# Residual of pairs 1 to 3 and the last pair's q/k transposes by DMA, with a frozen job order

## The chip, the core and the metric

The kernel runs on one core of one Trainium2 chip. The metric is the device time of one execution in microseconds (us); most executions of one kernel agree within about 1% here. TensorE does the matrix products, VectorE (DVE), ScalarE (ACT) and GpSimd (POOL) the elementwise work, SyncE (SP) issues nearly all DMA transfers. TensorE's work is in two forms: 128x128 tiles for the dense layers and four 64x64 tiles for attention.

## The reference

```python
# attention without softmax: batch 8, heads 8, sequence 576, head size 64
scores = q @ k^T / sqrt(64)
out    = (scores * D_h) @ v        # D_h[t,s] = gamma_h**(t-s) for t>=s, else 0
x = out with heads side by side    # 8 x 576 x 512
# gated layer
h = gelu(x @ w_in)                 # 512 -> 1024
u, v = two halves of h
v_n = layernorm(v) * g_ln
v_s = w_sg @ v_n + b_sg            # product along the sequence, 576 x 576
result = x + (u * v_s) @ w_out     # the residual is this "x +"
```

All inputs and the output are float32; the kernel works in bfloat16 on TensorE.

## The kernel before

The eight batches are handled as four **pairs**, a pair as nine row tiles of 128 rows, hence 36 output tiles. Attention goes through five blocks per pair (four of 256 rows, one of 128), 20 in all, and carries a state from block to block. For each block: transposes of q and k (job T), scores (S), state (Z) and attention output (O), which gives `xT`, the transposed x. For each row tile: the v half (hv) and the u half (hu) of the first dense layer; for each batch the spatial product with `w_sg` (wp); for each tile the output product (op).

Every piece is a job with an engine, an estimated duration and a due time. A planner in Python places them when the program is built: on each engine it takes, of the jobs that can start at about the earliest time, the one that is due first. The chip then runs each engine strictly in that order.

```python
    def a_OS(b, g):                      # attention output of block b, with scores of the next in it
        a_O(b, st.pop((b, "zs")))
        cur.pop("mark", None)
        if g is None:
            nc.tensor.drain()
        else:
            a_S(b + 1, g)
            nc.tensor.drain()
        cur.pop("mark", None)
        a_O2(b)                          # the last 8 matmuls, into banks that the first part also writes

    def m_U(i):                          # one tile, 16 matmuls of N=128
        ...
        for c in range(KK):
            for kk in range(KK):
                nc.tensor.matmul(hu[:, c, :], w_in[:, kk, 128 * c:128 * c + 128],
                                 xTs[p][:, kk, 128 * m:128 * m + 128],
                                 start=(kk == 0), stop=(kk == KK - 1), skip_group_check=True)

    def m_O(i):                          # output tile i
        ...
        for j in range(KK):              # the residual: xT transposed back by a product with the identity
            nc.tensor.matmul(o6[:, j // 2, :, j % 2, :], xTs[p][:, j, r], ident[:].rearrange("p (c d) -> p c d", c=2),
                             start=(j == 0), stop=False, skip_group_check=True)
        for c in range(KK):
            nc.tensor.matmul(op[:], gTs[p][:, c, r], w_out[:, c, :], start=False, stop=(c == KK - 1),
                             skip_group_check=True)

    def m_Oev(i):
        nc.scalar.activation(cur["ob", i][:], cur.pop(("op", i))[:], Act.Copy)
    ...
    loads(0)                             # q, k, v of block 0
    jv = [win_load(1, 0), win_load(1, 1)]
    ju = [win_load(0, 0), win_load(0, 1)]
    loads(1)
    loads(2)
    sg = [sg_load(j) for j in range(SB)]
    loads(3)
    wo = [wo_load(0), wo_load(2)]
    for b in range(4, NBL):
        loads(b)
```

## Time and profile before

| before | value |
|---|---|
| first three timed runs, median (range) | 241.68 us (240.2 to 243.03) |
| span of the profiled run | 239.6 us |
| TensorE busy | 215.4 us, 90% |
| first wp | 61.32 us |
| first wp to last matmul | 61.3 to 235.8, 174.5 us |

The busy times of the engines, the stretches of 20 us, the chain and the middle of TensorE's timeline are shown in the prediction below. What it does not show is the DMA part of the page; the second line is packets, MB and the time of the packets as a share of 16 engines' span:

```profile
DMA packets 70765, 42.92 MB, mean 179 GB/s; under 512 B 14817, under 2 KB 63993, under 8 KB 70721
...
q1 hardware_dynamic: 70176, 42.26, 63.4%
```

To read: over the span the main queue fills 63% of the DMA engines' time. That average hides how full they are at each time: 0.89 to 1.05 in the stretches up to 80 us, 0.12 to 0.15 from 160 to 220 us.

### The profile page before, as it was taken

What the parts mean: (1) busy time and instruction counts of PE and PEld (TensorE: products, weight loads), DVE (VectorE), ACT (ScalarE), POOL (GpSimd) and SP (SyncE); (2) the same over time, 40 slices, a digit from 0 to 9 for tenths busy, and PEclk for the clock granted to TensorE, in tenths of its full rate; (3) what the DMA queues carried; (4) which work ended last, traced back from release to release, by engine and by line L of the source; (5) the groups of instructions that cost most, each with busy time, mean ns of one, the idle gap of its engine ahead of it and who ended that gap; (6) DMA issues with size and microseconds to landing.
All of it is one profiled execution on the core that took longest, in us unless ns stands there. A gap on an engine that the chain in (4) does not pass through costs nothing.

```text
span 239.6 us, 10051 instructions
## 1 busy us (share of the span) xinstructions
PE 215.4 (90%) x4440; PEld 148.0 (62%) x4485; DVE 137.1 (57%) x230; ACT 135.1 (56%) x234; POOL 126.8 (53%) x198
## 2 busy tenths in 40 slices
PE   7975839887989999999999999899999999999993
PEld 2442617654766676677676667566757666667761
DVE  7991626665765745665667466374756555634420
ACT  2027247865656475576645665767473656865422
POOL 8955645499595569772437497906083802221000
PEclk9999989999999999999999999999999999999998
DMA  6999589999899985898564658971110220111324
GB/s 177 251 237 259 138 260 328 290 277 267 176 302 280 310 219 149 244 294 238 149 196 137 193 140 253 298 198 47 48 47 11 80 94 34 59 47 44 131 92 175
DMA packets 70765, 42.92 MB, mean 179 GB/s; under 512 B 14817, under 2 KB 63993, under 8 KB 70721
## 3 DMA queue, kind: packets, MB, share of 16 engines
q1 hardware_dynamic: 70176, 42.26, 63.4%
q8 instruction: 35, 0.57, 1.1%
q10 hardware_dynamic: 544, 0.02, 0.2%
q14 instruction: 10, 0.07, 0.1%
HBM read 32.80 MB, written 9.44 MB: 176 GB/s over the span
## 4 chain that ended last, share of the span: by engine, by line
PE 76%; DMA 13%; issue 4%; ACT 3%; SPq 1%; POOL 1%; ACTq 0%
PE wp L575 17%; PE hu L559 13%; PE op L596 13%; PE hv L517 12%; PE pp L439 7%; DMA ld<-in_q_dram 4%; PE pp L367 4%; PE pp L393 4%; PE op L593 3%; DMA ld<-in_moe_w_out_dram 3%; DMA ld<-in_moe_w_in_dram 3%; PE zp L421 3%; DMA ld<-in_moe_w_sg_dram 2%; ACT xT L506 1%; PE scr L248 1%
## 5 line engine op out<-in xcount | busy, mean ns | idle before, releaser
L403 DVE TENSOR_TENSOR ret<-pp,msk 128x1024 bf16<-128x1024 f32 x32 | 38.9, 1220 | 27.8 <-PE pp L393 27.6
L350 POOL TENSOR_TENSOR qkb<-ld,gqv 128x512 bf16<-128x512 f32 x36 | 37.1, 1051 | 15.6 <-DMA ld<-in_q_dram 12.9
L350 POOL TENSOR_TENSOR vb<-ld,gqv 128x512 bf16<-128x512 f32 x36 | 38.2, 1081 | 5.8 <-DMA ld<-in_v_dram 3.6
L575 PE MATMUL wp<-wT,vn 128*128 128x288 bf16 x256 | 41.2, 286 | 0.0
L582 DVE TENSOR_TENSOR gT<-wp,uT 128x288 bf16<-128x288 f32 x64 | 28.7, 453 | 21.0 <-PE wp L575 20.8
L533 POOL TENSOR_SCALAR mv<-mv 128x2 f32<-128x2 f32 (+1 forms) x20 | 4.5, 226 | 67.5 <-DVE mv L529 48.9
L559 PEld LDWEIGHTS <-w_in 128*128 128x128 bf16 x576 | 34.4, 98 | 6.9 <-issue 0.3
L559 PE MATMUL hu<-xT,w_in 128*128 128x128 bf16 x576 | 38.3, 219 | 0.2 <-issue 0.2
L517 PE MATMUL hv<-w_in,xT 128*128 128x512 bf16 x122 | 35.6, 380 | 2.6 <-ACT xT L506 1.4
L528 DVE BATCH_NORM_STATS2 bst<-vg 128x6 f32<-128x512 f32 x36 | 24.8, 690 | 19.3 <-ACT vg L521 19.3
L596 PE MATMUL op<-w_out,gT 128*128 128x512 bf16 x127 | 33.4, 379 | 0.9
L521 ACT ACTIVATE vg<-hv 128x512 f32<-128x512 f32 x36 | 21.5, 596 | 20.3 <-PE hv L517 18.1
L600 ACT ACTIVATE ob<-op 128x512 f32<-128x512 f32 x36 | 21.4, 595 | 19.4 <-PE op L596 19.4
L372 DVE COPY qkT<-pp 128x2048 bf16<-128x2048 bf16 (+1 forms) x20 | 22.2, 1111 | 15.1 <-PE pp L367 15.1
L565 ACT ACTIVATE uT<-hu 128x512 bf16<-128x512 f32 x36 | 21.5, 596 | 15.6 <-PE hu L559 15.6
L548 ACT ACTIVATE vn<-vg,mv 128x512 bf16<-128x512 f32 x32 | 25.0, 809 | 8.8 <-POOL mv L536 8.7
L506 ACT ACTIVATE xT<-pp 128x512 bf16<-128x512 f32 (+1 forms) x40 | 24.6, 665 | 8.2 <-PE pp L439 8.2
L575 PEld LDWEIGHTS <-vn 128*128 128x128 bf16 x256 | 23.9, 98 | 6.7
L517 PEld LDWEIGHTS <-xT 128*128 128x128 bf16 x144 | 12.6, 98 | 13.1 <-ACT xT L506 2.4
L341 POOL CAST qkb<-ld 128x1024 bf16<-128x1024 f32 (+1 forms) x20 | 19.5, 975 | 0.5 <-DMA ld<-in_k_dram 0.5
L248 PE MATMUL scr<-warm 128*128 128x512 bf16 x61 | 17.6, 436 | 2.2 <-DVE warm L221 1.2
L421 PE MATMUL zp<-vb,qkb 64*64 64x64 bf16 x480 | 13.8, 194 | 6.1 <-ACT zb L427 4.4
(66 smaller groups left out, 263.9 us busy)
## 6 DMA issues: line engine op xcount, KB each, us to landing
out_dram<-ob SPq DMA_DIRECT2D x36, 256.0 KB, 2.7
ld<-in_q_dram SPq DMA_DIRECT2D x16, 512.0 KB, 5.5
ld<-in_k_dram SPq DMA_DIRECT2D x16, 512.0 KB, 6.9
ld<-in_v_dram SPq DMA_DIRECT2D x16, 512.0 KB, 8.1
ld<-in_moe_w_in_dram SPq DMA_DIRECT2D x8, 256.0 KB, 7.0
ld<-in_moe_w_sg_dram SPq DMA_DIRECT2D x4, 288.0 KB
ld<-in_q_dram SPq DMA_DIRECT2D x8, 128.0 KB, 5.1
ld<-in_k_dram SPq DMA_DIRECT2D x8, 128.0 KB, 3.6
```

What stands on the lines that cost most here:

```text
L350: nc.gpsimd.tensor_tensor(dst[:, s], src[:, s], gqv[:, a, 2 * n + s, :].unsqueeze(2).to_broadcast([128, H, D]), op=Alu.mult)
L372: nc.vector.tensor_copy(st[b, "qkT"][:].rearrange("p c a k t -> p c (a k t)")[:, :, :w], st.pop((b, "tp"))[:].rearrange("p c a k s t -> p ...
L403: nc.vector.tensor_tensor(ret[:].rearrange("p r (k t) -> p (r k) t", k=2), sc[:].rearrange("p r (k t) -> p (r k) t", k=2), msk2[:].rearran ...
L506: nc.scalar.activation(dst, src, Act.Copy)
L517: nc.tensor.matmul(hv[:], xTs[p][:, kk, 128 * m:128 * m + 128], w_in[:, kk, F2:], start=(kk == 0), stop=(kk == KK - 1))
L521: nc.scalar.activation(vgs[i][:], cur.pop(("hv", i))[:], Act.Gelu_apprx_tanh)
L528: nc.vector.bn_stats(bst[:], vgs[i][:])
L548: nc.scalar.activation(vn[:], vg[:], Act.Identity, scale=mv[:, s, 2:3], bias=mv[:, s, 3:4])
L559: nc.tensor.matmul(hu[:, c, :], w_in[:, kk, 128 * c:128 * c + 128], xTs[p][:, kk, 128 * m:128 * m + 128], start=(kk == 0), stop=(kk == KK ...
L575: nc.tensor.matmul(ps[:], vns[t0 + j][e][:, 128 * c:128 * c + 128], wT[e][j][:, half * HS:(half + 1) * HS], start=(j == 0), stop=(j == SB ...
L582: nc.vector.tensor_tensor(gTs[p][:, c, col:col + HS], cur.pop(("wp", b, c, half))[:], uTs[p][:, c, col:col + HS], op=Alu.mult)
L596: nc.tensor.matmul(op[:], gTs[p][:, c, r], w_out[:, c, :], start=False, stop=(c == KK - 1), skip_group_check=True)
```

## The change

The intent is to take work off TensorE. The residual of pairs 1 to 3 (27 of 36 tiles) no longer goes through TensorE: a DMA transpose turns `xT` back and VectorE adds it as it evacuates the output product. The q/k transposes of the last pair (blocks 15 to 19) become DMA transposes too. Around this, the drain in the attention output is replaced by a wait on another job, hu is 256 wide, the start is rearranged, and the planner's greedy choice is replaced by a fixed list of 921 jobs (and seven groups of filler, matmuls on a tile of zeros) that stands in the kernel's text. The planner's time model now counts instruction fetch.

```diff
+FETCH = (7200.0, 4800.0)
+ORDER = (
+    '0 f9 1 2 6 111 83 7 f10 84 112 3 8 114 113 f5 115 17 87 81 118 120 278 116 9 279 119 12 280 f7 281 88 121 117 '
+    ... (33 lines)
+)
     def plan(self):
+        if ORDER:
+            return self.follow(ORDER)
...
-    BUFS = dict(ld=9, qkb=2, vb=3, qkT=2, ret=4, zb=4, xT=2, uT=2, gT=2, vg=3, mv=3, vn=10, ob=3,
+    BUFS = dict(ld=12, wst=2, qkb=2, vb=3, qkT=3, ret=4, zb=4, xT=2, uT=2, vg=3, mv=3, vn=10, ob=3, xr=3,
+    XP = 1          # from this pair on the residual goes by DMA
+    TB = 15         # from this block on q and k are transposed by DMA
...
+    def win_load(half):              # was four loads of 512 KB, in shared buffers, each issued in two halves
+            nc.sync.dma_start(wst["in", half][:, :, :F2],
+                              moe_w_in.rearrange("(j p) f -> p j f", p=128)[:, :, half * F2:(half + 1) * F2])
...
+    def a_TX(b):
+        st[b, "qkT"] = new("qkT", [128, 2048], BF)
+        nc.sync.dma_start_transpose(st[b, "qkT"][:, :ns * 1024].rearrange("p (g t) -> p g t", t=128),
+                                    st[b, "qkb"][:, :ns * 1024])
...
     def a_O2(b):
+        on = pend.pop(b)
+        if on is None:
+            nc.tensor.drain()
+        elif on:
+            nc.tensor.wait_ge(swap, on)      # set by a matmul of a job that the order put between a_O and a_O2
...
     def m_O(i):
+        if p < XP:
+            for j in range(KK):
+                ins = nc.tensor.matmul(op[:, 128 * j:128 * j + 128], xTs[p][:, m, j, :], ident[:], ...)
         for c in range(KK):
+            ins = nc.tensor.matmul(op[:], uTs[p][:, c, r], w_out[:, c, :], start=(p >= XP and c == 0), ...)
+    def m_X(i):
+        cur["xr", i] = new("xr", [128, KK, 128], BF)
+        nc.sync.dma_start_transpose(cur["xr", i][:], xTs[p][:, m].rearrange("p j r -> p (j r)"))
     def m_Oev(i):
+        if i // NT < XP:
+            ins = nc.scalar.activation(ob[:], op[:], Act.Copy)
+        else:
+            ins = nc.vector.tensor_tensor(ob[:], op[:], cur.pop(("xr", i))[:].rearrange("p j r -> p (j r)"), op=Alu.add)
...
-    jv = [win_load(1, 0), win_load(1, 1)]
-    ju = [win_load(0, 0), win_load(0, 1)]
-    loads(1)
+    jv = win_load(1)
+    loads(1)
+    ju = win_load(0)
     loads(2)
```

Left out: the planner's new duration model, the row constants (now through TensorE instead of four partitions of VectorE and small DMAs), the memsets that move to VectorE, and q and k of block 0 prepared by VectorE and ScalarE instead of GpSimd.

## The prediction

> **What bounds the kernel now.** I read the page's parts 1 and 2 first, then busy time in stretches of 20 us, then TensorE's timeline in the filled middle and in the first 62 us, then the chain of waits that ended last, for the start only.
>
> The engines over the whole span (busy us, share, instructions), and from the costliest groups the one that the change's name aims at:
>
> ```profile
> PE 215.4 (90%) x4440; PEld 148.0 (62%) x4485; DVE 137.1 (57%) x230; ACT 135.1 (56%) x234; POOL 126.8 (53%) x198
> ...
> L593 PE MATMUL op<-ident,xT 128*128 128x128 bf16 x144 | 13.9, 219 | 0.0
> ```
>
> TensorE is the only engine near full; the others stand at 53 to 57%. The 219 ns of one matmul is its length in the pipeline, not its cost.
>
> The same by stretches (busy us of 20 per engine, TensorE's granted clock, DMA share, GB/s):
>
> ```profile
> 0.00:20.00 20.00, 17.22 (x219) 8.26 (x223) 16.93 (x31) 4.62 (x7) 14.07 (x31) 1.00 0.99 230
> 20.00:40.00 20.00, 12.35 (x307) 8.63 (x309) 7.91 (x14) 10.90 (x19) 11.06 (x14) 0.91 0.89 230
> ...
> 100.00:120.00 20.00, 19.55 (x398) 13.53 (x402) 11.90 (x20) 14.22 (x24) 10.46 (x17) 1.00 0.80 239
> 120.00:140.00 20.00, 19.33 (x475) 13.96 (x480) 12.37 (x22) 11.79 (x22) 11.52 (x17) 1.00 0.54 156
> ...
> 160.00:180.00 20.00, 19.44 (x425) 13.82 (x427) 11.96 (x20) 12.17 (x21) 9.25 (x15) 1.00 0.12 43
> ```
>
> There are two regimes. Up to about 60 us the DMA engines are full and TensorE is not; of its 17.22 us in the first stretch most is filler (61 recorded matmuls on "warm", 17.6 us in all) that only keeps the clock up. From 60 us on TensorE is 97% busy and the DMA engines fall to 0.12.
>
> The chain that ended last, at the start (start us, length, what):
>
> ```profile
> 3.16 7.15 DMA ld<-in_moe_w_in_dram
> 10.31 0.02 issue
> 10.33 10.50 DMA ld<-in_q_dram
> ...
> 27.32 5.44 DMA ld<-in_moe_w_sg_dram
> ...
> 37.62 7.39 DMA ld<-in_moe_w_out_dram
> ...
> 53.33 1.43 issue
> ```
>
> The second block's q lands only at 20.83, behind 2 MB of w_in. The first spatial product (wp, "W") starts at 61.32 in TensorE's timeline. By then TensorE has done 7 hv jobs, 7 hu jobs, transposes of 5.5 blocks, the transposes of w_sg and their small products. At the filled-middle costs below that is about 28 us of work in 61 us: 33 us are lost at the start.
>
> The filled middle, TensorE alone (start, length with overlap, what):
>
> ```profile
> 110.45 0.39 PE L593 MATMUL op<-ident,xT 128*128 128x128 bf16 x4
> 110.68 1.03 PE L596 MATMUL op<-w_out,gT 128*128 128x512 bf16 x4
> 111.54 1.06 PE L559 MATMUL hu<-xT,w_in 128*128 128x128 bf16 x16
> 112.44 0.65 PE L575 MATMUL wp<-wT,vn 128*128 128x288 bf16 x4
> 112.92 0.29 PE L575 MATMUL wp<-wT,vmid 128*128 128x288 bf16 x1
> 113.14 0.31 PE L439 MATMUL pp<-qkT,zb 64*64 64x128 bf16 x8
> ```
>
> What counts is start to start: residual 110.45 to 110.68, 0.23 us; output product 0.86; hu 0.90; the five wp some 0.61; then about 0.1 is lost as the array turns from 128x128 to 64x64 tiles. One pair of batches takes 50.0 us: the same hv job starts at 95.90, 145.07 and 195.89.
>
> **What the Trainium skill says.** (1) "TensorE: Matmul & The Clock Gate", section "Back-to-back issue gap", gives a warm gap of N/2.4 + 2.5 ns: 56 ns at N=128, 216 at N=512. The trace agrees: 0.23 us for four of N=128, 0.86 for four of N=512. So making hu 256 wide instead of 128 should save nearly nothing in streaming (0.89 us per unit either way). (2) "DMA: Bandwidth & Descriptors", section "Latency and other measured facts", gives a DMA transpose 261 GB/s. No run before this change has such a DMA. (3) "Runtime: NRT & Kernel Launch", section "Instruction fetch mechanics": instructions come in blocks of 256 (16 KiB), the crossing "mostly hidden". The trace has 35 packets on the instruction queue, and 8972 TensorE instructions / 256 = 35.05: the count agrees. That it is hidden is less clear: at 53.33 TensorE stands for 1.43 us for "issue", in the middle of one job with the DMA engines full.
>
> **The change, part by part.** Counts are from the two instruction orders (8972 TensorE rows before, 6701 after).
>
> a) Residual. Of 36 output tiles 27 lose 4 matmuls: 27 x 0.23 = 6.2 us off TensorE, all in the filled part. In return 27 DMA transposes of 128 KB, and VectorE adds and evacuates instead of ScalarE. An estimate from skill place (2): 128 KB / 261 GB/s = 0.5 us, 13.5 us of DMA time in all, mostly after 110 us where the DMA share was 0.54 and less. VectorE takes 27 evacuations, estimated at 0.65 us from ScalarE's 0.60 for the same tile: +17.5 us; it loses 5 qkT evacuations (-5.5) and the 4-partition row arithmetic of the start (about -10, given back in part by memsets that move to it): roughly 144 us, no bound. ScalarE loses 27 x 0.595 = 16 us.
>
> b) q and k of the last pair. Four full blocks and a half one: 4.5 x 0.52 us (119.97 to 120.49 is one full set) = 2.3 us off TensorE. Their DMA transposes move 2.36 MB, an estimated 9 us at 261 GB/s.
>
> c) No more drain behind each attention output. Before, the output job, scores in the drain's shadow and the last 8 matmuls took 101.85 to 103.18 = 1.33 us; their columns alone, 4 tiles at a time at 2.4 GHz, are 0.85. Some 0.23 of the rest is the two turns of the array, so about 0.25 is drain. The new order puts another job (T, Z or S) there and waits on a semaphore of that job. 17 jobs in the filled part x 0.25 = 4.2 us.
>
> d) Fewer turns between 64-wide and 128-wide work: 106 before, 78 after by the orders. 28 x 0.11 = 3.1 us, of which about 2.4 in the filled part.
>
> e) The start. w_in comes as two 1 MB loads behind q and k of the second block, q and k of block 0 are prepared by VectorE and ScalarE beside GpSimd, the row constants go through TensorE instead of DVE on 4 partitions and tiny DMAs, the staging has buffers of its own. In the new order the first wp stands behind the transposes of block 4. q and k of block 4 are the 20th load; by then some 9.8 MB have been asked for. At the 230 GB/s of the first 40 us, from 2 us on, they land near 44 us; preparing them takes GpSimd 3 us (1.04 + 2.04 in the trace); then come about 4.5 us of TensorE work. That gives 49 to 51 us for the first wp; I take 49.5, against 61.3. This is the largest and least sure term: 11.8 us.
>
> The sum. From the first wp to the last matmul before: 61.3 to 235.8 = 174.5 us. Minus 6.2 (a), 2.3 (b), 4.2 (c), 2.4 (d); plus 1.9 because half the w_sg transposes and one set of q/k transposes now come after the first wp: 161.3. 49.5 + 161.3 = 210.8; plus the tail after the last matmul, unchanged (235.8 to 239.6 = 3.8): a span of 214.6. The timed median was 2.1 above the profiled span (241.7 against 239.6): 216.7, rounded to **216**.
>
> **Rivals.**
>
> *The DMA engines become the bound.* Up to 160 us the old run used about 141 us of full DMA time (the shares of eight stretches). Ahead of the last load the new queue has 15 stores, 9 residual transposes and 2.5 q/k transposes: some 149 us by the estimates above. The last block's scores are needed about 176 us in, by counting 32 us of TensorE work behind the last attention output. For: 149 of some 165 is tight, and I have no measured time of a DMA transpose; at half the page's rate it is 158. Against: the queue was idle a third of 100 to 140 us. It would cost 5 to 10 us: 222 to 226.
>
> *The start is bound by arrivals anyhow.* If first wp stays near 57 us, because loads of the same bytes take as long, the gain there is 4 us and the time 224. Against: of the 61 us, several are order (a zp job waited 4.07 us behind a ScalarE cast that waited for w_sg), not bytes.
>
> *A fixed order that fits badly.* The job order is a frozen list; where the chip differs from the author's durations each engine still waits in order, and TensorE stalls on evacuations. VectorE and ScalarE at 65% leave room, but I would give up 3 to 6 us: 219 to 222.
>
> *Better than summed.* 2271 fewer TensorE instructions, so 26 fetched blocks for 35, could remove most of the "issue" stalls, and the new start may overlap more: 208 to 211.
>
> **Range and chances.** The removals in the filled part (15 us) rest on measured spacings and I trust them to 4; the start to 6 either way; the DMA rival pulls up only. So 216, 208 to 226 in 8 of 10. Even if the whole start gain failed, 241.7 - 13 = 229 would be over 5% faster; only a DMA queue that is badly blocked makes it same. Faster 0.96, same 0.03, slower 0.01.
>
> **What would show it.** No residual matmul in 27 tiles, and a pair (same hv job to same hv job) at about 46 us, 44 in the last. The first wp near 49.5 us. TensorE idle under 1 us per 20 in the filled part, with no DMA named as releaser of the added matmul or of VectorE's output add. Transposes near 0.5 us of 16 engines each. A DMA share near 1 still at 160 us, or TensorE waiting for qkT or GpSimd for ld late, would say the first rival; waits spread over evacuations the third. Wrong overall if first wp is later than 56 us or a pair takes over 48.

## The result, and the profile after

| | before | changed |
|---|---|---|
| timed, median (range), 4 runs each | 240.94 us (238.7 to 243.03) | 214.78 us (213.73 to 215.84) |
| span of the profiled run | 239.6 us | 213.9 us |
| first wp | 61.32 us | 45.43 us |
| last matmul ends | 235.8 us | 209.3 us |
| DMA transposes | none | 27 of 128 KB, 4 of 512 KB, 1 of 256 KB |

The ratio is 0.8951, interval 0.8875 to 0.9027: faster. All ratios here are the mean time of one kernel's fast runs over that of the other's of the same rounds, so not quite the ratio of the medians quoted. Medians and ranges take in every execution, slow ones too; the ratios do not. Where a difference of ratios is given in us, it is multiplied by the median of the kernel before in the same rounds.

Two repeats in later sets gave 0.902 and 0.9026. The mean of the three, 0.8999, is called the **pooled ratio** below. It is needed for the first set of experiments, which has no run of the changed kernel; the three values come from different chips, and from the lowest to the highest of them is 1.8 us.

The page of the changed kernel: engines, DMA packets and the main queue, the new add on VectorE, and the two DMA transposes (median us from issue to landing).

```profile
PE 199.7 (93%) x3372; PEld 133.7 (63%) x3372; DVE 141.3 (66%) x261; ACT 123.2 (58%) x214; POOL 113.5 (53%) x157
...
DMA packets 94117, 48.64 MB, mean 227 GB/s; under 512 B 38202, under 2 KB 87362, under 8 KB 94082
...
q1 hardware_dynamic: 94064, 48.13, 93.9%
...
L771 DVE TENSOR_TENSOR ob<-op,xr 128x512 f32<-128x512 f32 x27 | 18.4, 689 | 11.9 <-PE op L755 11.4
...
xr<-xT SPq DMA_TRANSPOSE x27, 2.8
qkT<-qkb SPq DMA_TRANSPOSE x5, 5.9
```

TensorE's recorded busy time fell by 15.7 us (3.5 of them filler, 17.6 to 14.1) and VectorE's rose by 4.2. The surprise is the queue: 93.9% of 213.9 us is 200.9 us of engine time, against 151.9 (63.4% of 239.6) before: 49 us more, for some 6 MB more. Packets under 512 B rose by 23,385. The transposes account for nearly all of them: in pieces of 256 bytes they make 27 x 512 + 4.5 x 2048 = 23,040, and counted by size the packets of 256 bytes went from 12,288 to 35,328, which is 23,040 more.

Busy time by stretches, in the columns of the prediction's table:

```profile
0.00:20.00 20.00, 18.16 (x240) 9.75 (x241) 12.78 (x39) 7.23 (x10) 9.59 (x23) 1.00 0.99 277
20.00:40.00 20.00, 17.73 (x376) 11.87 (x373) 13.27 (x24) 17.32 (x33) 12.91 (x16) 1.00 1.09 267
...
100.00:120.00 20.00, 18.16 (x429) 13.06 (x427) 14.09 (x25) 11.76 (x22) 12.64 (x17) 1.00 0.92 248
120.00:140.00 20.00, 18.59 (x327) 12.79 (x320) 13.54 (x25) 11.33 (x20) 13.43 (x18) 1.00 1.18 220
140.00:160.00 20.00, 18.50 (x303) 12.09 (x302) 13.45 (x24) 10.91 (x20) 11.96 (x13) 1.00 1.10 195
```

Two things to see. In the first 40 us the DMA moves 277 and 267 GB/s, not the 230 of before. And from 100 to 160 us TensorE is idle for 4.75 us while the DMA share stands at 0.92 to 1.18 (it can pass 1 because the packets' times overlap).

Of those 4.75 us, 4.71 are three stalls, in TensorE's timeline (in brackets the idle time and what ended it; "issue" means that the profile shows nothing it waited for):

```profile
104.01 0.27 PE L595 MATMUL pp<-qkT,zb 64*64 64x128 bf16 x3 [1.84 <-issue]
...
127.14 1.02 PE L662 MATMUL hv<-w_in,xT 128*128 128x512 bf16 x4 [1.41 <-ACT uT L719]
...
155.39 0.32 PE L542 MATMUL pp<-qkT 64*64 64x64 bf16 x16 [1.46 <-DMA qkT<-qkb]
```

The third is a DMA transpose of q and k that came late. The first two name no DMA; whether they hang on one is for the experiments. In the two repeats the three stalls were 0.9 (two stalls together) and 0.7 for "issue", 1.4 and 1.4 for ScalarE, 1.3 and 0.5 for the transpose; the idle time from 100 to 160 us was 3.58 and 3.40 us.

SyncE's timeline shows a second cost, the time that an issue takes:

```profile
147.70 3.04 SPq L518 DMA_TRANSPOSE qkT<-qkb  x1
150.78 0.58 SPq L430 DMA_DIRECT2D ld<-in_k_dram  x1
151.48 3.42 SPq L764 DMA_TRANSPOSE xr<-xT  x1
```

A 128 KB transpose holds SyncE's queue for at least 1.19 us in this run (3.42 here) and a 512 KB one for 3.0 to 4.3. A plain transfer can be held up too (2.97 us for the load of q at 41.66), but the shortest store takes 0.34 us and the shortest load 0.37. Whatever stands behind a transpose in the order is issued that much later. From 120 to 160 us SyncE is issuing for 36.4 of 40 us, against 12.2 in the kernel before.

The start, in the chain that ended last:

```profile
26.64 6.93 DMA ld<-in_v_dram
...
37.26 1.86 POOL qkb L462
39.13 1.00 POOL qkb L456
...
40.17 0.64 PE pp L502 x32
...
45.59 1.23 PE wp L728 x10
```

Block 4's q and k are prepared from 37.2 us on and GpSimd does not wait for them: they were there. TensorE transposes them at 40.17; 5.3 us later the first wp starts at 45.43 (the chain's piece begins a little after it).

Last, the drain, in TensorE's timeline:

```profile
46.88 0.62 PE L595 MATMUL pp<-ret,vb 64*64 64x128 bf16 x32
47.43 0.64 PE L502 MATMUL pp<-ident,qkb 64*128 64x64 bf16 x32
48.00 0.31 PE L595 MATMUL pp<-qkT,zb 64*64 64x128 bf16 x8
```

Between the output's 40 matmuls and its last eight (48.00) lies a transpose job, and the last eight follow it without a bracket.

### The profile page after: what moved, and what is told of

Same layout as the page of the kernel before. It is cut to its first block, busy times and chain, and to the rows that moved or that the text cites. A ratio compares the mean times of both kernels' runs of the same rounds, so it can differ in the third digit from the quotient of the medians.

```text
span 213.9 us, 7830 instructions
## 1 busy us (share of the span) xinstructions
PE 199.7 (93%) x3372; PEld 133.7 (63%) x3372; DVE 141.3 (66%) x261; ACT 123.2 (58%) x214; POOL 113.5 (53%) x157
## 3 DMA queue, kind: packets, MB, share of 16 engines
q1 hardware_dynamic: 94064, 48.13, 93.9%
## 4 chain that ended last, share of the span: by engine, by line
PE 75%; DMA 7%; ACT 6%; POOL 4%; DVE 4%; issue 2%; SPq 0%; POOLq 0%; DVEq 0%
PE wp L728 16%; PE op L755 13%; PE hu L709 12%; PE hv L662 12%; PE pp L595 5%; PE scr L340 5%; DMA qkT<-qkb 4%; PE pp L542 3%; DMA ld<-in_v_dram 3%; PE pp L502 3%; PE zp L574 3%; ACT xT L651 2%; PE op L750 1%; DVE ret L555 1%; DVE ob L771 1%
## 5 line engine op out<-in xcount | busy, mean ns | idle before, releaser
L462 POOL TENSOR_TENSOR vb<-ld,gqv 128x1024 bf16<-128x1024 f32 (+1 forms) x20 | 34.6, 1731 | 14.2 <-DMA ld<-in_v_dram 14.2
L462 POOL TENSOR_TENSOR qkb<-ld,gqv 128x1024 bf16<-128x1024 f32 (+1 forms) x19 | 32.7, 1723 | 15.9 <-PE zp L574 11.8
L738 DVE TENSOR_TENSOR uT<-wp,uT 128x288 bf16<-128x288 f32 x64 | 27.9, 449 | 18.9 <-PE wp L728 18.8
L709 PE MATMUL hu<-xT,w_in 128*128 128x256 bf16 (+1 forms) x320 | 37.3, 262 | 0.7 <-ACT xT L651 0.7
L662 PE MATMUL hv<-w_in,xT 128*128 128x512 bf16 x144 | 36.4, 380 | 1.4 <-ACT uT L719 1.4
L755 PE MATMUL op<-w_out,uT 128*128 128x512 bf16 x144 | 35.9, 379 | 0.3 <-DVE uT L738 0.3
L709 PEld LDWEIGHTS <-w_in 128*128 128x128 bf16 x320 | 27.9, 98 | 7.6 <-issue 0.9
L719 ACT ACTIVATE uT<-hu 128x512 bf16<-128x512 f32 x36 | 21.2, 596 | 12.3 <-PE hu L709 12.2
L771 DVE TENSOR_TENSOR ob<-op,xr 128x512 f32<-128x512 f32 x27 | 18.4, 689 | 11.9 <-PE op L755 11.4
L583 ACT ACTIVATE zb<-zp 128x256 bf16<-128x256 f32 x32 | 12.2, 380 | 15.4 <-PE zp L574 15.2
L755 PEld LDWEIGHTS <-uT 128*128 128x128 bf16 x144 | 13.3, 98 | 12.4 <-DVE uT L738 0.9
L511 DVE COPY qkT<-pp 128x2048 bf16<-128x2048 bf16 (+1 forms) x15 | 16.7, 1113 | 6.3 <-PE pp L502 6.1
```

Source lines behind the costliest of these rows:

```text
L462: eng.tensor_tensor(dst, src, g.unsqueeze(3).to_broadcast(list(src.shape)), op=Alu.mult)
L662: ins = nc.tensor.matmul(hv[:], xTs[p][:, m, kk, :], w_in[:, kk, F2:], start=(kk == 0), stop=(kk == KK - 1))
L709: ins = nc.tensor.matmul(hu[:, n, :], w_in[:, kk, 128 * c:128 * c + 128], xTs[p][:, m:m + w, kk, :], start=(kk == 0), stop=(kk == KK - 1), ...
L719: unfence(nc.scalar.activation(uTs[p][:, c0:c1, 128 * m:128 * m + 128 * w], cur.pop(("hu", i, half))[:], Act.Gelu_apprx_tanh), ("U", i, half))
L738: ins = nc.vector.tensor_tensor(uTs[p][:, c, col:col + HS], cur.pop(("wp", b, c, half))[:], uTs[p][:, c, col:col + HS], op=Alu.mult)
L755: ins = nc.tensor.matmul(op[:], uTs[p][:, c, r], w_out[:, c, :], start=(p >= XP and c == 0), stop=(c == KK - 1), skip_group_check=True)
```

## The experiments

Twelve runs in three sets, each set timed beside the kernel before on one chip, but each set on another one (medians of the kernel before: 242.87, 241.23 and 240.11 us). The theory: the order and the start carry most of the gain; the residual by DMA is not free, because the DMA queue has no room where the order puts it. The rival: the parts that the title lists (residual and transposes by DMA) give the gain and the order is a detail.

### The residual without its DMA

```diff
     def m_X(i):
-        cur["xr", i] = new("xr", [128, KK, 128], BF)
-        nc.sync.dma_start_transpose(cur["xr", i][:], ...)
+        return
     def m_Oev(i):
-            ins = nc.vector.tensor_tensor(ob[:], op[:], cur.pop(("xr", i))[:]..., op=Alu.add)
+            ins = nc.vector.tensor_tensor(ob[:], op[:], warm[:], op=Alu.add)     # warm is zero
```

> The changed kernel without its 27 residual transposes and without residual matmuls for these tiles (VectorE adds a tile of zeros instead: a wrong result on purpose, same VectorE work). Theory A, TensorE sets the pace and the DMA transposes are hidden: same as the changed kernel, 214 to 215 us, since no TensorE work changes. Theory B, the DMA queue is a second bound (share 0.94 over the span, above 1 in most stretches to 160 us): the transposes' share goes and 2 to 6 us with it, 209 to 213 us.

Measured: median 212.0 us (210.91 to 212.62), ratio 0.8752, interval 0.868 to 0.8825. Results are wrong, as meant. Its page and its stretches:

```profile
q1 hardware_dynamic: 79376, 44.59, 79.3%
```

```profile
100.00:120.00 20.00, 20.00 (x440) 14.24 (x439) 15.94 (x26) 13.27 (x25) 14.52 (x17) 1.00 1.05 284
120.00:140.00 20.00, 19.89 (x342) 13.41 (x344) 13.62 (x25) 12.80 (x21) 11.98 (x18) 1.00 0.72 168
140.00:160.00 20.00, 20.00 (x372) 14.18 (x361) 14.25 (x28) 11.62 (x21) 14.79 (x17) 1.00 0.88 211
```

TensorE's idle time from 100 to 160 us falls from 4.75 to 0.11 us; all three stalls are gone. So all three hang on the 27 transposes, though only one named a DMA. Against the pooled ratio the transposes cost (0.8999 - 0.8752) x 242.87 = 6.0 us (4.8 to 6.7 by the lowest and highest of its three values). In DMA engine time, 79.3% of 208.8 is 165.6 us; 200.9 - 165.6 = 35.3 us more with the 27, **1.31 us for each one added**. That is the rise of the total, with what they do to the other packets' times, and not the time of one transpose by itself. The chain of cause can begin early: with the transposes, pair 1's first ones are issued from 66.9 us on, and between 86 and 96 us the DMA share is 0.98 where it is 0.71 without them; so the loads of the next blocks start from a queue that is already full. By how much the stalls come from engine time and by how much from the issue time on the queue, this run does not tell: it takes both away.

### The transposes doubled

```diff
     def m_X(i):
+        again = new("xr2", [128, KK, 128], BF)
+        nc.sync.dma_start_transpose(again[:], xTs[p][:, m].rearrange("p j r -> p (j r)"))
```

> Each of the 27 residual transposes is issued a second time, into a tile that nobody reads: 27 more of 128 KB. A (hidden): at most +1 us, 214 to 216. B (second bound): the added DMA time shows, +4 to +15 us, 219 to 230. The difference of the DMA queue's total busy time against the changed kernel also measures what one transpose costs: 0.5 us of 16 engines if the skill's 261 GB/s holds, about 1 us if my reading of the two traces is right.

Measured: 236.88 us (234.54 to 237.47), ratio 0.9767, interval 0.9675 to 0.9859. That is (0.9767 - 0.8999) x 242.87 = 18.7 us over the changed kernel, for 27 transfers whose results nobody reads, and more than the 4 to 15 us that theory B expected. Between 120 and 140 us:

```profile
120.00:140.00 20.00, 15.59 (x262) 9.99 (x262) 10.14 (x18) 10.77 (x20) 13.79 (x19) 0.91 0.95 181
```

The first 27 cost 6.0 us and the second 27 cost 18.7. Here the profile does name transposes: VectorE's output add waits 7.5 us for them in all, and ScalarE waits 4.7 us for one before it writes a new xT (there are two buffers), with TensorE 4.5 us behind it. Not all of that is waiting: TensorE's busy time rose from 199.7 to 206.8 us, 7.1 us, at a mean granted clock of 0.954 instead of 0.996 (0.91 in the stretch shown). The run was also to measure one transpose, 0.5 or about 1 us. The main queue takes 92.8% of 235.3 = 218.4 us, 17.5 more than 200.9, so **0.65 us for each one added**, half of what the removal gave. A quiet stretch agrees: from 181 to 184 us of the changed kernel the queue moves one transpose and one 256 KB store, and is 45.6% busy, 1.37 us for the two together. So 1.31 us is what a transpose adds in this kernel's full queue, not a fixed cost. SyncE is now issuing for 16 to 19 of every 20 us from 100 to 220 us, 77.8 us of the run for these 54. So the issue time on the queue is a suspect beside the engines' time; the two are not told apart.

### The residual back on TensorE

```diff
-    BUFS = dict(ld=12, ... xT=2, ...)
+    BUFS = dict(ld=11, ... xT=3, ...)         # the order needs xT longer; one load buffer pays for it
     def m_O(i):
-        if p < XP:
+        if p < NP:                             # residual matmuls in all 36 tiles
     def m_X(i):
+        return
     def m_Oev(i):
-            ... tensor_tensor(ob[:], op[:], xr, op=Alu.add)
+            ... tensor_copy(ob[:], op[:])
```

> Residual of all pairs back on TensorE by 4 matmuls, no residual DMA, same job order, VectorE still evacuates (one more xT buffer, one load buffer less, else the order deadlocks). A: 27 x 0.225 = +6.1 us, 220 to 222. B: the relief of the DMA queue gives part back, +0 to +4 us, 214 to 219.

Measured: 217.05 us (215.94 to 218.47), ratio 0.8969, interval 0.8886 to 0.9052. TensorE is busy 205.9 us of 213.9 (96%), and never idle from 100 to 160 us. The residual on TensorE costs (0.8969 - 0.8752) x 242.87 = 5.3 us over no residual at all; by DMA it costs 6.0. Within the intervals they are equal: **in this order, the change that gives the kernel its name is worth nothing measurable for the residual.** What TensorE saves in work it stands idle. Two buffer counts differ too, so a small effect of those is in the figure.

### The last pair's transposes back on TensorE

```diff
-    TB = 15
+    TB = 20
-    ORDER = (...)
+    ORDER = (...)      # the same, with 5 transpose jobs and 5 evacuations put in about 3 us ahead of the scores
```

> q and k of the last pair transposed by TensorE again (4.5 block transposes of 0.57 us put about 3 us ahead of the block's first scores, VectorE evacuates 5 more tiles), no DMA transposes of q and k; the rest of the order as in the changed kernel. A: +2.6 us of matmuls and up to 5 pairs of array turns of 0.23: +2.5 to +4 us, 217 to 219. B: the 1.46 us stall for a q/k transpose and the queue's pressure go: -1 to +1.5 us, 213.5 to 216.

Measured: 220.69 us (218.42 to 221.91), ratio 0.9085, interval 0.8982 to 0.9187: (0.9085 - 0.8999) x 242.87 = 2.1 us slower than the pooled ratio, where 2.3 was predicted; it lies between the two expectations. The intervals overlap, so this is not clear of noise. Its profile fell in a slow execution (mean clock 0.977). As a rough reading of the queue alone, 81.2% of 220.2 is 178.8 us, and (200.9 - 178.8) / 4.5 = 4.9 us less for each 512 KB block, against an estimated 2; like the 1.31, this is a difference of totals in a full queue, here from a slow run.

### The changed kernel again, twice

No edit. The first is the partner of the three runs that follow, the second of the last three.

> The changed kernel itself once more, so that the others are compared on one chip: 213 to 217 us. Against it the residual on TensorE (217.05 in the earlier set) can be read; if this stands at 215 or more, the residual transposes earn at most 2 us in this order.

> The changed kernel a third time, as the base for the other three of this set: 213 to 217 us.

Measured: 216.88 us (215.54 to 218.62), ratio 0.902, interval 0.8944 to 0.9097; and 215.95 us (215.12 to 218.0, six runs), ratio 0.9026, interval 0.8976 to 0.9077. The first wp was at 45.42 and 45.96. The gain repeats; sets differ by under 1%.

### The frozen order taken away

```diff
-ORDER = ( ... )
+ORDER = ''            # plan() falls back to the greedy choice
```

> All parts of the change, but the frozen job order taken out, so that the planner's own greedy rule orders the jobs. If the removed work alone carries the gain (TensorE full whatever the order): 215 to 218. If the order carries a good part, at the start above all: 220 to 230, with the first spatial product several us later than 45.4.

Measured: 241.18 us (239.48 to 241.78), ratio 1.0003, interval 0.992 to 1.0086, far above the 220 to 230 expected. **The same operations as the changed kernel in the greedy order run as long as the kernel before, within the interval.** TensorE's waits (us in total, times, longest) and the first wp in its timeline:

```profile
PE hv L628 <- ACT xT L617: 4.8, 8, 1.2
PE pp L561 <- DVE ret L521: 2.8, 4, 1.1
PE zp L540 <- POOL vb L428: 2.7, 2, 1.5
PE wp L694 <- ACT vn L663: 2.6, 2, 2.2
```

```profile
52.27 0.66 PE L694 MATMUL wp<-wT,vn 128*128 128x288 bf16 x4
```

The first wp comes 9 us sooner than before, yet from there to the end of the span it takes 187.8 us (240.1 - 52.27), where the kernel before takes 178.3 and the changed one 168.5. The waits are spread over evacuations and preparations by all three other engines. Of the 26.2 us between this span and the changed kernel's, idle time makes 16.3; the other 9.9 are TensorE's own busy time, 209.6 us for 199.7, at a mean granted clock of 0.951 for 0.996. The greedy rule also places the filler matmuls itself (28 recorded in both kernels). One caution: the rule has constants (due times, penalties), and the record does not say whether they were tuned for this content without the frozen list. What is shown is that this content in that order gains nothing, not that no greedy order could.

### The named change alone, on the kernel before

```diff
 # on the kernel before; xT laid out tile by tile, drain, order rule, loads and start untouched
-        for j in range(KK):
+        for j in range(KK if p == 0 else 0):
             nc.tensor.matmul(o6[...], xTs[p][:, m, j, :], ident...)
+    def m_X(i): ...            # DMA transpose as in the changed kernel
     def m_Oev(i):
+        for a in range(2):     # pairs 1 to 3: two adds per tile on VectorE
+            nc.vector.tensor_tensor(ob5[:, a], op5[:, a], xr5[:, a], op=Alu.add)
```

> The kernel before with one part of the change alone: residual of pairs 1 to 3 by DMA transpose, VectorE adds (two instructions a tile, for its other column order). By the prediction's term: 27 x 0.225 = -6.1 us, 235 to 237 us where before stands at 241 to 243, because its DMA queue has room from 100 us on. If the transposes' contention costs what it cost in the changed kernel (about 4.8 us): 240 to 243, no gain.

Measured: 235.2 us (233.64 to 236.01), ratio 0.977, interval 0.9698 to 0.9842: (1 - 0.977) x 241.23 = 5.5 us gained, close to the 6.2 that the prediction's term (a) counts. Its queue stands at 81.3% of 234.3 us. One thing is mixed in: the greedy rule places every job anew when durations change, so the 5.5 us are not the residual's work alone.

The same step is worth 5.5 us in one kernel and about nothing in the other. The engine time that it adds is no smaller here, (190.5 - 151.9) / 27 = 1.43 us each; that it matters less because less else is wanted at the same time is my reading, not shown.

### The drain put back

```diff
     def a_O(b):
         ...
+        a_O2(b)                 # at once, so with a drain; the job that used to do it does nothing
```

> The last 8 matmuls of every attention output go straight behind its first part again, after a drain, as in the kernel before; the job that the changed kernel puts between follows. Prediction's term c: 17 to 20 x 0.25 us = +4 to +5 us, 218 to 221. Rival: that the semaphore wait of the changed kernel costs as much as the drain: +0 to +1.5.

Measured: 218.76 us (216.79 to 219.72), ratio 0.9084, interval 0.9005 to 0.9163: (0.9084 - 0.902) x 241.23 = 1.5 us slower than the changed kernel of the same set, 2.1 against the pooled ratio. The intervals overlap, so this is not clear of noise; term (c) counted 4.2. The edit is not quite the old arrangement either: in the kernel before, scores of the next block stand in front of the drain, here nothing does.

### The residual of six tiles back on TensorE

The changed kernel issues 11 of its 27 residual transposes before 160 us. The first six of them, from 66.9 to 137.0 us, go back to TensorE; the other five, from 138.9 to 160.0, stay.

```diff
     def m_O(i):
-        if p < XP:
+        if p < XP or NT <= i < NT + 6:       # first six tiles of pair 1
     # and the same condition in m_X (no transpose) and m_Oev (copy instead of add)
```

> An attempt at a better version: the residual of the first 6 tiles of pair 1, whose transposes run while the DMA queue is full, back on TensorE; the other 21 by DMA; same order and buffers. If transposes in the full stretch cost more than 0.2 us of TensorE each: -1 to -3 us against the changed kernel. If they are hidden there: +1.2 us (6 x 0.2).

Measured: 212.76 us (211.75 to 214.0, six runs), ratio 0.8879, interval 0.8835 to 0.8924; the changed kernel in the same rounds has 0.9026. That is 3.5 us faster, a little more than expected, and the intervals do not touch. It is correct, and **it beats both kernels**.

```profile
100.00:120.00 20.00, 19.79 (x446) 14.46 (x448) 15.80 (x27) 13.11 (x24) 14.27 (x18) 1.00 1.04 274
120.00:140.00 20.00, 19.79 (x331) 14.08 (x334) 14.06 (x25) 12.25 (x22) 13.13 (x18) 1.00 0.95 175
140.00:160.00 20.00, 19.80 (x319) 13.58 (x320) 14.27 (x26) 10.99 (x21) 14.25 (x15) 1.00 1.02 222
```

Six tiles of extra work on TensorE (about 1.4 us at 0.23 each) remove 4.1 us of its idle time in these 60 us (4.75 to 0.62; 2.8 against the 3.40 of the changed kernel in the same set). The DMA share is still 0.95 to 1.04 there, with the other five transposes in it, so a full queue does not always make the stalls. Which six are taken out, and how many, was not varied. In engine time the six took (198.7 - 187.8) / 6 = 1.8 us each off the same set's changed kernel.

### All of w_in first

```diff
-ORDER: ... 6 7 3 8 17 9 ...      # w_in half, q and k of block 1 ahead of the other half
+ORDER: ... 3 9 6 7 8 17 ...      # both halves of w_in ahead of block 1 (only SyncE's own list changes)
```

> Only the order of the first loads as in the kernel before: both halves of w_in ahead of the second block's q, k and v. If the early start comes from asking for q and k of block 1 before w_in: the first spatial product moves from 45.4 to 48 to 52 us and the time by +3 to +6 us. If what counts is only how many bytes come ahead of block 4 (my prediction's reasoning: the same in both): first product within 1 us of 45.4, time +0 to +1.

Measured: 221.27 us (220.4 to 226.64), ratio 0.9218, interval 0.9144 to 0.9292: (0.9218 - 0.9026) x 240.11 = 4.6 us slower. The first wp moves to 52.19, 6.2 us later than the 45.96 of the same set's repeat. The first line of TensorE's waits:

```profile
PE pp L503 <- POOL qkb L457: 6.5, 1, 6.5
```

TensorE stands 6.5 us for block 1's k. The DMA moves as fast as in the changed kernel (278 and 261 GB/s in the first two stretches), so the order of the loads is worth about 4.6 us, by what arrives first and not by the rate. That answers the prediction's way of counting too: the bytes ahead of block 4 are the same in both.

### Block 0 on GpSimd alone

```diff
-        eng = nc.vector if b == 0 and t == "q" else nc.gpsimd
+        eng = nc.gpsimd
-            if b == 0: nc.scalar.activation(dst, src, Act.Copy)      # k
+            nc.gpsimd.tensor_copy(dst, src)
```

> Only q and k of block 0 prepared by GpSimd again instead of by VectorE and ScalarE. The first transposes come some 3 us later (9.0 to 12), but if arrivals of the loads set the start, the first spatial product stays within 1 us of 45.4 and the time within 1 us; if the start is a chain of compute from block 0 on: +2 to +3 us.

Measured: 218.28 us (216.5 to 220.08), ratio 0.9086, interval 0.9022 to 0.915: 1.4 us slower, between the two expectations, intervals overlapping. Its first wp is at 49.24, but that profile fell in a slow execution, so I do not read a size from it.

## Why the prediction was right or wrong

The time (216 against 214.8 measured), the direction and the range held. That the number was so close is partly luck, as errors cancelled: of the predicted span of 214.6, the start came 4.1 us better (45.4 for 49.5), the filled part 2.6 worse (163.9 for 161.3) and the tail 0.8 worse (4.6 for 3.8), which gives 213.9. (The working's 216.7 would round to 217, and TensorE's share from 60 us on is 96%, not 97; neither matters. Place (1) left out that the page calls its gap that of a single matmul and gives other spacings for a stream; in this trace the stream follows the single gap, 0.23 and 0.86 us for four.) The filled part is luckier than it looks. Of the 10.6 us by which it shrank, the experiments find about nothing for (a), some 2 for (b) and 1.5 to 2.1 for (c). The other 6 or so are in no measured term; the fixed order is the candidate, as the greedy run suggests.

**(e) The start: right as the largest term, too small.** The number that was mis-sized is the rate: "At the 230 GB/s of the first 40 us, from 2 us on, they land near 44 us". The changed kernel moves 277 and 267 GB/s, and block 4's q and k are being prepared at 37.2. After that the 3 us on GpSimd and the TensorE work (5.3 us for my 4.5) are as predicted. But counting bytes at a rate is not enough: with w_in first, the same bytes at the same rate give a first wp at 52.19, because TensorE waits 6.5 us for block 1, and the greedy order has its first wp at 52.27 with 278 and 264 GB/s. Why the rate is higher was not tested. The form of the transfers differs (w_in in two transfers instead of eight, no 4-partition transfers, staging of their own), and any of these may be it.

**(a) The residual: the step that failed, the room in the queue.** The 6.2 us off TensorE is real, 5.3 by experiment. What failed is "0.5 us, 13.5 us of DMA time in all, mostly after 110 us where the DMA share was 0.54 and less". There is no such room: from 120 to 160 us the share is 1.18 and 1.10, since loads and transposes now meet there. In that full queue the 27 add 35.3 us of engine time, not 13.5, though by the doubling (0.65 us each) and the quiet stretch the 0.5 is not far off for one transpose by itself. The prediction also gave no cost to the time that SyncE needs to issue them. So 6.0 us of stalls pay for the 5.3 and the net is about nothing. VectorE's part was right (0.689 us for 0.65, 141.3 us in total for 144).

**(b) q and k of the last pair: not contradicted**, 2.1 for 2.3, but with overlapping intervals, and with some 4.9 us of added engine time per block where I had 2.

**(c) The drain: most likely mis-sized.** 1.5 to 2.1 us instead of 4.2, not clear of noise. A drain that I put at 0.25 us in each of 17 jobs is worth some 0.1, or the other jobs' order absorbs the rest.

**(d) The turns between tile forms** (2.4 us) were not tested by themselves.

**The rivals.** *DMA as the second bound* came true in part: a share over 0.9 to 160 us, and TensorE waiting for qkT, both marks that the prediction had named. But it took 6 us off the gain rather than making the kernel slower than predicted, because the start gave more. *A frozen order that fits badly* was the wrong way round: without the frozen order there is no gain at all. My sum of terms treated the order as given and credited each removal; the greedy run shows that the same removals gain nothing in that order. *Better than summed* is what the six-tile kernel makes of it, at 212.76 us. The mark "a pair at about 46 us" cannot be read: the new order is not periodic.

**Issue stalls.** The prediction let fewer fetched instruction blocks remove most of them. 26 packets instead of 35 came as counted, but one stall of 1.84 us was still there, 0.7 to 0.9 in the repeats, none without the transposes and 0.2 at most with six fewer; the greedy order has one of 1.5. That they follow fetches delayed by a full DMA fits but was not tested.

## What to carry to other kernels

In this kernel, work moved from the busiest engine to the DMA queue was not free: where the queue was full it cost as much as it saved, and with the first six tiles left on TensorE the kernel is 3.5 us faster than with all 27 moved. So measure such a transfer's engine time and issue time under the load that it will meet (here 0.65 to 1.8 us of engine time for the same 128 KB), then move it part by part. And when a change comes with a new instruction order, run the new operations under the old ordering rule before you credit them: here they gained nothing under it, and a wait's named releaser did not tell which transfer was behind it, while taking that transfer away did.

## What the Trainium skill lacked or had wrong

- "DMA: Bandwidth & Descriptors", section "Latency and other measured facts", gives a DMA transpose 261 GB/s, from one kernel. Here 128 KB of bfloat16 from SBUF to SBUF added between 0.65 us of the 16 engines (200 GB/s, by doubling the transposes) and 1.31 us (100 GB/s, by removing them from a full queue). The page's figure for a transpose does not say how it falls beside other transfers.
- The same page's section "DMA Transpose (X-bar)" lists constraints but no duration for which a transpose holds its issuing queue; elsewhere the page has only cycle counts for unnamed earlier generations. Here it was at least 1.19 us for 128 KB and mostly 3.0 to 4.3 us for 512 KB, against 0.34 and 0.37 us for the shortest plain store and load. With the transposes doubled, SyncE issued for 16 to 19 of every 20 us from 100 to 220 us.
- "Runtime: NRT & Kernel Launch", section "Instruction fetch mechanics": the count of one packet per 256 instructions agrees (35 and 26 packets for 8972 and 6701). Whether the crossing is "mostly hidden" stays open here: stalls of 1.43 us before and 1.84 us after, for which the profile names no releaser, stand where the DMA share is over 1; that the fetch is their cause was not tested.
